# Down-weight sums from GpSimd to VectorE, gated layers' norms from VectorE to ScalarE, token sums pair by pair

## The chip, the cores and the metric

The kernel runs on one core of one Trainium2 chip. The metric is the device time of one execution in microseconds (us). The engines that appear are TensorE (PE, with its weight loads as PEld), VectorE (DVE), ScalarE (ACT), GpSimd (POOL) and SyncE (SP), which issues most transfers. A row of the trace that says L663 belongs to line 663 of the kernel before.

## What is computed

Four layers stand on a residual stream x of 2048 tokens with 1024 features. Layers 0 and 2 are linear attention, layers 1 and 3 are gated feed-forward layers; both kinds use the same two sets of weights. Each layer takes a layer norm of x and adds its result to x.

```
def _layernorm(x, axis=-1, eps=1e-5):          # (x - mean) / sqrt(var + eps)

A:  q, k, v = heads(x @ wqkv)                  # 32 heads of 32
    pq, pk = phi(q), phi(k)                    # t + 1 where t > 0, else exp(t); + 1e-6
    kv = einsum(pk, v);  z = sum(pk)
    o  = einsum(pq, kv) / (einsum(pq, z) + 1e-6)
    return o @ wo

B:  gate = x @ W_gate;  up = x @ W_up          # 1024 -> 3584
    h = relu(gate) * up
    return h @ W_down                          # 3584 -> 1024

x = x + A(layernorm(x));  x = x + B(layernorm(x))
x = x + A(layernorm(x));  x = x + B(layernorm(x))
```

## The kernel before

Tokens are 16 tiles of 128 (t = 0 to 15), four tiles to a quarter. x stays in SBUF in fp32.

**Attention layers** (`layer_A`). After the projections and the key-value product comes the out stage: for each tile and each half of the columns `out_unit` (line 544) runs eight matmuls into a PSUM bank (one of four), and VectorE adds the result to x (line 555). During the out units of quarters 1 and 2 the norms of the next layer's first two quarters are prepared: `ln_at` (line 344) queues, step by step, two statistics on VectorE (line 154), their aggregate (line 159), two short operations on ScalarE for 1/sqrt (lines 161 and 162), the scaling of the whole 128 x 1024 tile on VectorE (`ln_scale`, line 170), and a transposing transfer on SP's queue (`ln_turn`, line 342).

**Gated layers** (`layer_B`). Tokens go in two chunks of eight tiles (c = 0, 1). The three big products use a block scheme with seven block products in place of eight (2 x 2 blocks): so sums of blocks are needed of the tokens (`sums_x`, lines 697 to 700, four VectorE operations for a pair of tiles), of the gate and up weights (`make_gu`, lines 663 to 666, three VectorE operations on a weight block) and of the down weights (`make_d`, lines 670 to 686, four GpSimd operations on a unit). The weights' sums are made once, in layer 1, chunk 0, and are stored to DRAM by transfers on ScalarE's queue (lines 667 and 684); chunk 1 and layer 3 load them.

A chunk has fourteen gate/up units (`glu`, line 708), each of fourteen groups of four matmuls, then one down stage (`down`, line 777). In a unit ScalarE copies products from PSUM (lines 741 and 745) and applies relu (line 732), VectorE joins them (lines 755, 758 and 735; zg and zu are the sums of line 755, on which the next matmuls accumulate), and GpSimd makes one product (line 762).

**Order.** `later.at(n, f)` queues f until n ticks on; a tick is one unit of matmuls in attention, one group of four in a gated layer. In the out stage the order on VectorE and GpSimd is the order of the code (line 599). Elsewhere a planner orders each engine's instructions in advance from estimated costs. Either way every engine and each transfer queue then runs its list strictly in order. SP's queue has the loads and transposes, ScalarE's queue has the stores of the sums. Large buffers come from one pool of 16 (`slot`, line 146): weight blocks in a ring, the token blocks, their sums, h, and the raw down weights with their sums; a load starts when an earlier user has released its buffer.

Of the kernel before, what the change touches and what calls it, by code (L numbers as in the profile page):

```python
# [8 lines left out]
ALU = mybir.AluOpType  # L9
ACT = mybir.ActivationFunctionType  # L10
F32 = mybir.dt.float32
BF16 = mybir.dt.bfloat16
F16 = mybir.dt.float16
PSUM = bass.MemoryType.PSUM
P = 128
NW = 512
HD = 32
QT = 4
# [71 lines left out]
class _Net:  # L90
# [71 lines left out]
        nc.scalar.activation(out=rstd, in_=rstd, func=ACT.Exp, scale=-0.5)  # L162
        return mv, rstd

    def ln_scale(self, src, mv, rstd, xn=None, h=None):
        if xn is None:
            xn = self.temp([P, self.D], F16, name="xnb")
        w = self.D // 2
        s = slice(None) if h is None else slice(h * w, (h + 1) * w)
        self.nc.vector.tensor_scalar(out=xn[:, s], in0=src[:, s], scalar1=mv[:, 0:1],  # L170
                                     scalar2=rstd[:, 0:1], op0=ALU.subtract, op1=ALU.mult)
        return xn

    def ln_norm(self, layer, t):

        nc = self.nc
        src = self.xb[t] if layer == 0 else self.x[t]
        stats = self.small.tile([P, 2, nc.vector.BN_STATS_DIM], F32, tag="stats")
        for c in range(2):
            self.ln_stat(t, src, c, stats)  # L180
        r = self.ln_rstd(stats)

        def scale():
            home = self.xn_home(layer, t) if layer % 2 == 0 else None
            return self.ln_scale(src, *r, home)

        return scale

# [209 lines left out]
    def layer_A(self, l, last_ln):  # L398
        nc, G, KT, D = self.nc, self.G, self.KT, self.D
        ring, later = self.ring, self.later  # L400
        H = D // NW
        heads = lambda a: a.rearrange("p (h d) -> p h d", d=HD)
        pq_of, pqT, T = {}, {}, []
# [52 lines left out]
        def m_units(d):  # L456
            mt = self.temp([P, D], BF16, name=f"mt{l}_{d}")
            for h in range(H):
                ps = self.ps3.tile([P, NW], F32, tag="b")
                for t in range(self.ST):  # L460
                    nc.tensor.matmul(ps, lhsT=self.xn[l, t][:, d * P:(d + 1) * P],  # L461
                                     rhs=self.pk[l, t][:, h * NW:(h + 1) * NW],
                                     start=(t == 0), stop=(t == self.ST - 1))
                    if t == self.ST // 2 - 1:
                        later.tick()
                nc.scalar.activation(out=mt[:, h * NW:(h + 1) * NW], in_=ps, func=ACT.Copy)
                if h == H - 1:
                    later.at(2, lambda: kv_step(d, mt))
                later.tick()
# [30 lines left out]
        def z_mult(sc, j):  # L500
            prod = sums[:, 1 - next(prods) % 2, :]
            nc.gpsimd.tensor_tensor(out=prod, in0=pq_of[sc, j], in1=zrow, op=ALU.mult)  # L502
            later.at(2, lambda: z_sum(prod, sc, j))
# [17 lines left out]
        def fold_wo(n):  # L521

            n2, a = divmod(n, H)
            if n2 == 0:
                T.append(self.slot(f"T{l}_{a}", [P, 4, D]))
            ps = [pool.tile([P, NW], F32, tag=tag, name=f"fold{l}_{n}_{i}") for i, (pool, tag) in
                  enumerate(((self.kvp, "kv0"), (self.kvp, "kv1"), (self.ps3, "b"), (self.ps3, "b")))]
            wo = ring.get((l, f"o{n2}"))
            for b in range(R):
                g = a * R + b  # L530
                for i in range(R):
                    e = slice(i * HD, (i + 1) * HD)
                    nc.tensor.matmul(ps[i][b * HD:(b + 1) * HD, :], lhsT=kvT[e, g, e],
                                     rhs=wo[e, g, :], start=True, stop=True,
                                     tile_position=(i * HD, b * HD))
            for i in range(R):
                g = a * R + i
                dst = T[g // 4][:, g % 4, n2 * NW:(n2 + 1) * NW]
                if g % 2:
                    nc.scalar.activation(out=dst, in_=ps[i], func=ACT.Copy)  # L540
                else:
                    nc.vector.tensor_copy(out=dst, in_=ps[i])
# [16 lines left out]
        def column_major(f, q):  # L559
            return [lambda j=j, c=c: f(q, j, c) for c in range(H) for j in range(QT)]  # L560

        def row_major(f, q):
            return [lambda j=j, c=c: f(q, j, c) for j in range(QT) for c in range(H)]

        def run(*lists):

            n = max(len(u) for u in lists)
            for i in range(n):
                for u in lists:
                    if i < len(u):  # L570
                        u[i]()
                        later.tick()
# [26 lines left out]
        with self.tc.manual_schedule(engines={mybir.EngineType.DVE, mybir.EngineType.Pool}):  # L599
            ring.free_before((l, "v0"))  # L600
            later.at(5, z_row)
            for i in range(11):
                later.at(7 + 2 * i, lambda i=i: z_mult(*divmod(i, QT)))
            for d in range(KT):
                m_units(d)
            if l > 0:
                later.at(1, lambda: [self.bring_back(t) for t in range(self.NS)])
            q3 = row_major(q_unit, self.NQ - 1)
            out0 = column_major(out_unit, 0)

            def with_fold(u, i):
                return lambda: (u(), fold_wo(i // 2) if i % 2 == 0 else None)

            run(q3[:2])
            run([with_fold(u, i) for i, u in enumerate(q3[2:] + out0[:1])])
            run(out0[1:3])
            ring.free_slowly((l, "o0"), later, 2)
            for i in range(11, self.ST):
                later.at(1 + 3 * (i - 11), lambda i=i: z_mult(*divmod(i, QT)))
            run(out0[3:])  # L620
            for sc in range(1, self.NQ):
                if sc < 3:
                    self.ln_later(last_ln, sc - 1, 1, 3, 2)
                run(row_major(out_unit, sc))


# [42 lines left out]

    def make_d(self, u):  # L670

        g = self.nc.gpsimd
        t = self.slot(f"wd{u}")
        raw = t[:, 0:4, :].rearrange("p (h n) f -> p h n f", h=2)
        T = t[:, 4:8, :].bitcast(F16)
        self.nc.sync.dma_start(out=raw, in_=self.wd_v[:, :, u, :].rearrange("p h (n f) -> p h n f", f=NW))

        def sums():
            for o, a, b in ((T[:, 0, :], raw[:, 0, 1, :], raw[:, 0, 0, :]),
                            (T[:, 1, :], raw[:, 1, 1, :], raw[:, 0, 1, :]),  # L680
                            (T[:, 2, :], raw[:, 1, 1, :], T[:, 0, :]),
                            (T[:, 3, :], raw[:, 1, 0, :], T[:, 2, :])):
                g.tensor_tensor(out=o, in0=a, in1=b, op=ALU.subtract)  # L683
            self.later.at(2, lambda: self.nc.scalar.dma_start(out=self.td[:, :, u, :], in_=T))

        self.later.at(6, sums)
# [155 lines left out]
    def layer_B(self, l, final):  # L842
        ring = self.ring
        for c in range(2):
            if c == 0:
                for j in range(QT):
                    self.sums_x(l, c, j)
            hT = []
            first = l == 1 and c == 0
            for u in range(self.U):  # L850
                if u % 2 == 0:
                    hT.append(self.slot(f"h{l}_{c}_{u // 2}", dtype=F16))
                ring.load_to(ring.index((l, c, "g", u)) + (4 if first else 5))
                if first:
                    if u == 0:
                        for w in "gu":
                            self.make_gu(ring.get((l, c, w, 0)), w, 0)
                    if u + 1 < self.U:
                        self.later.at(4, lambda u=u: [self.make_gu(ring.get((l, c, w, u + 1)), w, u + 1)
                                                      for w in "gu"])  # L860
                    self.make_d(u)
                self.glu(l, c, u, hT)
            if c == 0:
                self.ln_chunk(l, 1, 20, 3, 3)
            elif not final:
                self.ln_later(l + 1, 0, 28, 6, 4)
            self.down(l, c, hT, final)
# [68 lines left out]
```

## Time and profile before

| | us |
|---|---|
| median of 3 runs (1545.25 to 1549.07) | 1545.67 |
| the profiled execution | 1544.92 |
| its span, first to last instruction | 1543.0 |
| out stage of layer 0 (180.63 to 247.27) | 66.64 |
| layer 1, chunk 0: gate/up (247.27 to 457.14) | 209.87 |
| layer 1, chunk 0: down (457.14 to 544.67) | 87.53 |
| layer 1, chunk 1: gate/up (544.67 to 713.88) | 169.21 |
| out stage of layer 2 (970.77 to 1032.08) | 61.31 |
| layer 3, chunk 0: gate/up (1032.08 to 1200.87) | 168.79 |
| layer 3, chunk 1: gate/up (1285.47 to 1454.69) | 169.22 |

A row of a group of instructions reads: line, engine, operation, result <- operands, partitions x elements and type, count, then busy us in total, mean ns of one, and the idle time of the engine before them with what ended it. A row of waits reads: engine and what it was about to run, <- what it waited for, then us in total, times, longest. A row of the timeline reads: start, length, engine, line, operation, count, and in brackets the idle time before it.

### The profile page before, as it was taken

To read this page: it belongs to the slowest core of one execution; us is meant where nothing else is said; L and a number is where in the kernel's file an instruction comes from. 1 tells how busy PE (TensorE), PEld (TensorE's weight loads), DVE (VectorE), ACT (ScalarE), POOL (GpSimd) and SP (SyncE) were. 2 spreads that over 40 slices of the span, in tenths; PEclk is the share of its full clock that TensorE was granted. 3 is DMA by queue.
4 is the path that set the end of the run, shared out by engine and by line. 5 is a ranking of instruction groups with operands and counts; after the bars stand their busy time and mean duration, and the time that the engine had idled before them with its cause. 6 is when DMAs were issued, how large, how long until landed. Compare 5 with 4: busy or idle time off the path is not lost.

```text
span 1543.0 us, 18575 instructions
## 1 busy us (share of the span) xinstructions
PE 1487.9 (96%) x6993; PEld 671.9 (44%) x7039; DVE 877.6 (57%) x1399; ACT 464.7 (30%) x875; POOL 349.3 (23%) x246
## 2 busy tenths in 40 slices
PE   9999988788999999999999999989999999999999
PEld 4444433333344444444444444434444444444444
DVE  7845699866666454337356554895334733344632
ACT  5851202233320033342027622123343102433300
POOL 1349244333440001000003377311000000000100
PEclk9999999999999999999999999999999999999999
DMA  9402447655665894444752116576443589444461
GB/s 273 96 28 55 131 69 209 204 174 183 203 202 177 259 326 136 147 150 144 236 136 41 55 21 169 138 181 201 150 150 127 175 221 311 151 137 142 143 205 41
DMA packets 295673, 242.91 MB, mean 157 GB/s; under 512 B 105504, under 2 KB 269600, under 8 KB 295584
## 3 DMA queue, kind: packets, MB, share of 16 engines
q1 hardware_dynamic: 278224, 214.07, 47.5%
q10 hardware_dynamic: 17360, 27.66, 5.0%
q8 instruction: 55, 0.90, 0.2%
q14 instruction: 34, 0.28, 0.0%
HBM read 186.65 MB, written 30.41 MB: 141 GB/s over the span
## 4 chain that ended last, share of the span: by engine, by line
PE 84%; DVE 10%; DMA 3%; issue 2%; POOL 1%; ACT 0%; ACTq 0%; DVEq 0%; SPq 0%; POOLq 0%
PE ps L426 14%; PE dy L807 9%; PE yg L724 9%; PE yu L724 9%; PE ps L461 7%; PE dv L807 6%; PE xu L724 5%; PE xg L724 5%; PE dx L807 5%; PE zg L724 3%; PE zu L724 3%; PE vg L724 3%; PE vu L724 3%; PE ps L548 2%; DVE x L555 1%
## 5 line engine op out<-in xcount | busy, mean ns | idle before, releaser
L724 PEld LDWEIGHTS <-w 128*128 128x128 f16 (+1 forms) x3136 | 308.3, 98 | 413.9 <-issue 46.4
L762 POOL TENSOR_TENSOR h<-m5u,m5g 128x512 f16<-128x512 f32 x56 | 72.1, 1288 | 750.9 <-DVE m5u L758 721.3
L426 PE MATMUL ps<-w,xnT 128*128 128x512 bf16 x1024 | 223.4, 379 | 0.2 <-ACT xnT L286 0.2
L807 PEld LDWEIGHTS <-h 128*128 128x128 f16 x1120 | 109.4, 98 | 132.3
L755 DVE TENSOR_TENSOR zg<-yg,m5g 128x512 f32<-128x512 f32 x56 | 39.1, 698 | 209.1 <-PE yg L724 209.1
L426 PEld LDWEIGHTS <-xnT 128*128 128x128 bf16 x1024 | 99.2, 98 | 120.1 <-issue 1.4
L724 PE MATMUL yg<-s,w 128*128 128x512 f16 x448 | 117.8, 386 | 20.5 <-DVE zg L755 20.5
L548 PE MATMUL ps<-T,pqT 128*128 128x512 bf16 x500 | 112.3, 379 | 10.4 <-DVE x L555 9.5
L724 PE MATMUL xg<-xnT,w 128*128 128x512 f16 x448 | 115.8, 380 | 5.1 <-ACT yg L745 5.1
L724 PE MATMUL xu<-xnT,w 128*128 128x512 f16 x448 | 115.0, 379 | 2.4 <-ACT yu L745 2.4
L724 PE MATMUL yu<-s,w 128*128 128x512 f16 x448 | 116.5, 383 | 0.0
L732 ACT ACTIVATE m5g<-m5g 128x512 f32<-128x512 f32 x56 | 35.2, 629 | 224.0 <-DVE m5g L758 203.7
L807 PE MATMUL dy<-w,h 128*128 128x512 f16 x448 | 98.0, 379 | 0.0
L807 PE MATMUL dx<-w,h 128*128 128x512 bf16 x436 | 96.7, 379 | 0.6
L161 ACT ACTIVATE rstd<-mv,eps 128x1 f32<-128x1 f32 x64 | 18.3, 291 | 254.5 <-DVE mv L159 237.6
L548 PEld LDWEIGHTS <-pqT 128*128 128x128 bf16 x512 | 49.7, 97 | 72.4 <-issue 13.8
L683 POOL TENSOR_TENSOR wd<-wd 128x512 f16<-128x512 bf16 x56 | 73.4, 1333 | 33.1 <-DMA wd<-in_B_W_down_dram 24.8
L741 ACT ACTIVATE m5g<-vg 128x512 f32<-128x512 f32 x56 | 33.4, 597 | 151.0 <-PE vg L724 70.3
L514 POOL TENSOR_TENSOR pq<-pq,den 128x1024 bf16<-128x1024 bf16 x32 | 61.6, 1930 | 71.8 <-DVE den L509 70.5
L154 DVE BATCH_NORM_STATS2 stats<-x 128x6 f32<-128x512 f32 (+1 forms) x120 | 76.7, 673 | 1.9 <-DMA x<-in_A_x_dram 1.5
L502 POOL TENSOR_TENSOR sums<-pq,kvc 128x1024 f32<-128x1024 bf16 x32 | 69.1, 2165 | 31.6 <-DVE pq L374 18.3
L443 POOL TENSOR_TENSOR sums<-sums,slab 128x512 f32<-128x512 f32 x46 | 53.9, 1179 | 78.2 <-DVE slab L374 60.9
(100 smaller groups left out, 1964.1 us busy)
## 6 DMA issues: line engine op xcount, KB each, us to landing
w<-in_B_W_gate_dram SPq DMA_DIRECT2D x56, 512.0 KB, 6.0
w<-in_B_W_up_dram SPq DMA_DIRECT2D x56, 512.0 KB, 5.3
w<-td SPq DMA_DIRECT2D x32, 896.0 KB, 4.6
w<-in_B_W_down_dram SPq DMA_DIRECT2D x24, 896.0 KB, 5.2
w<-tg SPq DMA_DIRECT2D x42, 512.0 KB, 7.1
w<-tu SPq DMA_DIRECT2D x42, 512.0 KB, 6.3
w<-in_A_wqkv_dram SPq DMA_DIRECT2D x10, 1024.0 KB, 6.9
tg<-w ACTq DMA_DIRECT2D x14, 512.0 KB, 3.1
```

The costliest lines, as they stand in the source:

```text
L154: self.nc.vector.bn_stats(out=stats[:, c, :], in_=src[:, c * fmax:(c + 1) * fmax])
L426: nc.tensor.matmul(by_row(ps), lhsT=self.xnT[l, l_q][:, kt, j * P:(j + 1) * P], rhs=w[:, kt, :].rearrange("p (b i d) -> p i b d", i=R, d=H ...
L443: nc.gpsimd.tensor_tensor(out=ksum[:, cols], in0=ksum[:, cols], in1=pk, op=ALU.add)
L461: nc.tensor.matmul(ps, lhsT=self.xn[l, t][:, d * P:(d + 1) * P], rhs=self.pk[l, t][:, h * NW:(h + 1) * NW], start=(t == 0), stop=(t == sel ...
L502: nc.gpsimd.tensor_tensor(out=prod, in0=pq_of[sc, j], in1=zrow, op=ALU.mult)
L514: nc.gpsimd.tensor_tensor(out=heads(pq), in0=heads(pq), in1=den[:, :].unsqueeze(2).to_broadcast([P, D // HD, HD]), op=ALU.mult)
L548: nc.tensor.matmul(ps, lhsT=pqT[sc][:, g, j * P:(j + 1) * P], rhs=T[g // 4][:, g % 4, n2 * NW:(n2 + 1) * NW], start=(g == 0), stop=(g == G ...
L683: g.tensor_tensor(out=o, in0=a, in1=b, op=ALU.subtract)
L724: nc.tensor.matmul(ps, lhsT=W[w][m][:, k, :], rhs=A[m][:, k, :], start=start and k == 0, stop=k == 3, skip_group_check=True)
L755: nc.vector.tensor_tensor(out=Z[w], in0=Y[w], in1=V[w], op=ALU.add)
L762: nc.gpsimd.tensor_tensor(out=h[:, 3, :], in0=V["u"], in1=V["g"], op=ALU.mult)
L807: nc.tensor.matmul(banks[j], lhsT=A(k)[:, j * P:(j + 1) * P], rhs=w[:, i, :], start=start and k == 0, stop=k == self.U - 1, skip_group_che ...
```

## The change

Three things are edited.

1. `make_d` makes its sums with three VectorE operations (the first one makes two blocks at once, 128 x 1024) in place of four GpSimd operations.
2. `ln_norm`: in layers 1 and 3, and for the first quarter of layer 2, the tile is scaled on ScalarE, in one activation with a scale and a bias per token. The bias, -mean / std, is one VectorE operation on 128 x 1 (tile `shift`). Layer 0 and the other tiles of layer 2 stay on VectorE.
3. The token sums of chunk 0 are queued in the out stage, one pair of tiles at a time, 3j + 6 ticks into quarter 2, where before all four followed the out stage. In layer 0 the sums of the first gate and up blocks are queued one tick into quarter 3. Both thereby get a place in VectorE's order as written in the code.

```diff
-    def ln_scale(self, src, mv, rstd, xn=None, h=None):
-        if xn is None:
-            xn = self.temp([P, self.D], F16, name="xnb")
+    def ln_scale(self, src, mv, rstd, xn, h=None):
...
-        r = self.ln_rstd(stats)
+        mv, rstd = self.ln_rstd(stats)
 
         def scale():
-            home = self.xn_home(layer, t) if layer % 2 == 0 else None
-            return self.ln_scale(src, *r, home)
+            if layer % 2 == 0 and (layer, t // QT) != (2, 0):
+                return self.ln_scale(src, mv, rstd, self.xn_home(layer, t))
+            xn = self.temp([P, self.D], F16, name="xnb") if layer % 2 else self.xn_home(layer, t)
+            shift = self.small.tile([P, 1], F32, tag="shift")
+            nc.vector.tensor_scalar(out=shift, in0=mv[:, 0:1], scalar1=rstd[:, 0:1], scalar2=-1.0,
+                                    op0=ALU.mult, op1=ALU.mult)
+            nc.scalar.activation(out=xn, in_=src, func=ACT.Identity, scale=rstd[:, 0:1],
+                                 bias=shift[:, 0:1])
+            return xn
...
             for sc in range(1, self.NQ):
                 if sc < 3:
                     self.ln_later(last_ln, sc - 1, 1, 3, 2)
+                if sc == 2:
+                    for j in range(QT):
+                        later.at(3 * j + 6, lambda j=j: self.sums_x(last_ln, 0, j))
+                if sc == 3 and l == 0:
+                    for w in "gu":
+                        later.at(1, lambda w=w: self.make_gu(ring.get((last_ln, 0, w, 0)), w, 0))
                 run(row_major(out_unit, sc))
...
     def make_d(self, u):
-        g = self.nc.gpsimd
+        v = self.nc.vector
...
         def sums():
-            for o, a, b in ((T[:, 0, :], raw[:, 0, 1, :], raw[:, 0, 0, :]),
-                            (T[:, 1, :], raw[:, 1, 1, :], raw[:, 0, 1, :]),
-                            (T[:, 2, :], raw[:, 1, 1, :], T[:, 0, :]),
-                            (T[:, 3, :], raw[:, 1, 0, :], T[:, 2, :])):
-                g.tensor_tensor(out=o, in0=a, in1=b, op=ALU.subtract)
+            v.tensor_tensor(out=T[:, 0:2, :], in0=raw[:, :, 1, :], in1=raw[:, 0, :, :], op=ALU.subtract)
+            v.tensor_tensor(out=T[:, 2, :], in0=raw[:, 1, 1, :], in1=T[:, 0, :], op=ALU.subtract)
+            v.tensor_tensor(out=T[:, 3, :], in0=raw[:, 1, 0, :], in1=T[:, 2, :], op=ALU.subtract)
             self.later.at(2, lambda: self.nc.scalar.dma_start(out=self.td[:, :, u, :], in_=T))
...
     def layer_B(self, l, final):
         ring = self.ring
         for c in range(2):
-            if c == 0:
-                for j in range(QT):
-                    self.sums_x(l, c, j)
...
                 if first:
-                    if u == 0:
-                        for w in "gu":
-                            self.make_gu(ring.get((l, c, w, 0)), w, 0)
                     if u + 1 < self.U:
```

## The prediction

> **What bounds the kernel now.** I read the page first, then busy time by stage, then TensorE's waits, then the order of work inside the slowest stage.
>
> ```profile
> span 1543.0 us, 18575 instructions
> PE 1487.9 (96%) x6993; PEld 671.9 (44%) x7039; DVE 877.6 (57%) x1399; ACT 464.7 (30%) x875; POOL 349.3 (23%) x246
> ```
>
> TensorE is busy 96% of the span, so only its gaps can be won. The busy time by stage says where they are (columns: stretch, its length, busy time of PE, PEld, DVE, ACT and POOL, granted clock, DMA share, GB/s). The stretches start at the first matmul of each stage: out stage of layer 0, gate/up of layer 1 chunk 0, its down stage, gate/up of layer 1 chunk 1, out stage of layer 2.
>
> ```profile
> 180.63:247.27 66.64, 57.12 (x269) 25.00 (x273) 62.92 (x105) 5.64 (x19) 21.67 (x12) 1.00 0.51 116
> 247.27:457.14 209.87, 180.94 (x782) 78.55 (x783) 147.45 (x200) 63.70 (x117) 83.60 (x65) 0.95 0.58 189
> 457.14:544.67 87.53, 84.51 (x388) 38.28 (x392) 51.25 (x95) 7.19 (x23) 2.33 (x2) 1.00 0.77 235
> 544.67:713.88 169.21, 169.21 (x785) 76.60 (x784) 72.14 (x107) 65.33 (x112) 17.85 (x14) 1.00 0.55 174
> 970.77:1032.08 61.31, 56.64 (x269) 25.02 (x273) 54.72 (x97) 5.65 (x19) 17.17 (x8) 1.00 0.49 111
> ```
>
> The same fourteen gate/up units take 169.2 us where the weights' sums are only loaded, and 209.87 us where they are made: 40.7 us lost. The two out stages lose 66.64 - 57.12 = 9.5 and 61.31 - 56.64 = 4.7 us, and there VectorE is the busy engine. The first down stage loses 3.0 us. Together 57.9 us: what this change could win at most. TensorE's waits in those stretches, first five rows in gate/up of chunk 0, then one row each in the out stage of layer 0 and in the down stage (from the waits of each stretch):
>
> ```profile
> PE yg L724 <- DVE zg L755: 20.5, 6, 4.4
> PE xg L724 <- ACT yg L745: 5.1, 5, 2.0
> PE vg L724 <- DVE s L697: 3.6, 1, 3.6
> PE xu L724 <- ACT yu L745: 2.4, 1, 2.4
> PE yu L724 <- DVE m5u L758: 0.9, 1, 0.9
> PE ps L548 <- DVE x L555: 5.6, 7, 2.5
> PE dv L807 <- DVE x L873: 2.8, 1, 2.8
> ```
>
> The wait for s ends at 247.27 and belongs to the out stage. The others of gate/up give 28.9 us; the remaining 40.7 - 28.9 = 11.8 us must be matmuls at a lower clock (0.95 in that stretch). One burst of this stage in order of time (start, length):
>
> ```profile
> 292.49 0.84 DVE L665 TENSOR_TENSOR w<-w 128x512 f16<-128x512 bf16 x1
> 293.00 10.92 POOL L683 TENSOR_TENSOR wd<-wd 128x512 f16<-128x512 bf16 x8
> ...
> 302.84 1.63 DVE L663 TENSOR_TENSOR w<-w 128x1024 f16<-128x1024 bf16 x1
> 304.50 0.43 DVE L665 TENSOR_TENSOR w<-w 128x512 f16<-128x512 bf16 x1
> 305.31 0.69 DVE L755 TENSOR_TENSOR zg<-yg,m5g 128x512 f32<-128x512 f32 x1
> 306.05 1.87 PE L724 MATMUL yg<-s,w 128*128 128x512 f16 x4 [4.36 <-DVE zg L755]
> 307.71 1.91 PE L724 MATMUL zg<-s,w 128*128 128x512 f16 x4
> ```
>
> While GpSimd makes the down sums of two units (293.0 to 303.9), VectorE's sums of the gate and up weights stretch (line 663 to 1.63 us); the first one after it takes 0.43 us. The operation that TensorE needs (zg) stands behind them, TensorE stops 4.36 us, and its next two groups of four matmuls start 1.66 us apart, where a unit's fourteen groups at 169.2 / 14 us are 0.86 apart. Over the whole run:
>
> ```profile
> L663 DVE TENSOR_TENSOR w<-w x28: 677/1316/1640, 178.8 to 433.4; 128x1024 f16<-128x1024 bf16 x28
> L665 DVE TENSOR_TENSOR w<-w x28: 400/771/1367, 179.8 to 434.1; 128x512 f16<-128x512 bf16 x28
> L683 POOL TENSOR_TENSOR wd<-wd x56: 1149/1328/1607, 241.8 to 456.7; 128x512 f16<-128x512 bf16 x56
> L762 POOL TENSOR_TENSOR h<-m5u,m5g x56: 1263/1270/1593, 259.4 to 1453.3; 128x512 f16<-128x512 f32 x56
> ```
>
> The rows give shortest, median and longest ns. The minima (0.68 and 0.40) are VectorE alone, the maxima are beside GpSimd.
>
> **Part 1: the down sums move to VectorE.** Removed are 56 GpSimd operations, 4 x 1.33 = 5.3 us a unit. Added are three on VectorE in the shapes of lines 663, 665 and 666: 0.68 + 0.41 + 0.41 = 1.50 us a unit (0.41 between the shortest, 0.40, and the 0.43 above), 21.0 in fourteen. The store of the result stays on ScalarE's queue and now waits for VectorE. What the gate and up sums cost in this stage now:
>
> ```profile
> L663 DVE TENSOR_TENSOR w<-w 128x1024 f16<-128x1024 bf16 x25 | 30.6, 1228 | 3.9 <-DMA w<-in_B_W_gate_dram 3.3 <-DMA w<-in_B_W_up_dram 0.5
> L666 DVE TENSOR_TENSOR w<-w 128x512 f16<-128x512 bf16 x25 | 22.0, 881 | 0.5
> L665 DVE TENSOR_TENSOR w<-w 128x512 f16<-128x512 bf16 x25 | 19.1, 767 | 0.3
> ```
>
> That is 71.7 us; alone they would take 25 x 1.50 = 37.5. So VectorE does 37.5 + 21.0 = 58.5 us of sums in place of 71.7: more work, 13 us less time, 147.45 - 13.2 = 134 us for a stage of 169 of TensorE. The burst shows what this does to the wait: from 292.49 to 305.31 VectorE ran three sums like line 663, eight of the short kind and one 0.68 operation, 12.8 us. Alone: 3 x 0.68 + 8 x 0.41 + 0.68 = 6.0, plus the down sums of two units, 3.0, makes 9.0. Zg comes 3.8 us sooner and 0.6 of the 4.36 us stay. With no long stop the lower clock goes too.
>
> What stays of the 40.7: six waits for zg at 0.5 = 3.0; half of the 7.5 us for the copies on ScalarE, which stand behind the issues of the stores (these wait for the sums) = 3.7; the lower clock, 1; and something new. A wait for the down weights' load, which held GpSimd alone, now holds VectorE, and behind it zg, the products into h and, through the stores, ScalarE's copies. In this stage GpSimd's row is 8.9 us:
>
> ```profile
> POOL wd L683 <- DMA wd<-in_B_W_down_dram: 8.9, 2, 8.7
> wd<-in_B_W_down_dram SPq DMA_DIRECT2D x12, 512.0 KB, 4.5
> td<-wd ACTq DMA_DIRECT2D x13, 512.0 KB, 3.7
> ```
>
> I take 6 of it, the rest meeting slack. Residue 14, so 27 us won. Bounds: all 40.7, or below nothing (the slower rival). One conflict stays: the product on GpSimd (line 762) meets VectorE's sums once a unit; I take it as hidden: by the code it follows the unit's last addition, and nine groups of matmuls, some 8 us, lie between that and the next zg. The Trainium skill's page SBUF — State Buffer, "Who interferes with whom" and the rule above it, says that the port pair VectorE and GpSimd share is an exclusive lock, so a two-input VectorE operation can stand for a whole GpSimd operation. By it the sum could lose up to what rival 4 works out, where mine loses nothing; the trace's worst stretch of line 663, 1.64 against 0.68 us, is less than such a full block.
>
> **Part 2: norms scaled on ScalarE.** The rows are line 170 in the out stages of layers 0 and 2, a ScalarE copy of the same width, and the nearest tiny operation:
>
> ```profile
> L170 DVE TENSOR_SCALAR xnb<-x,mv,rstd 128x1024 f16<-128x1024 f32 x8 | 12.0, 1496 | 0.2
> L170 DVE TENSOR_SCALAR xnb<-x,mv,rstd 128x1024 f16<-128x1024 f32 x8 | 10.1, 1257 | 0.2
> L448 ACT ACTIVATE e<-sums 128x1024 bf16<-128x1024 f32 x2 | 2.1, 1047 | 0.0
> L508 DVE TENSOR_SCALAR den<-den 128x32 f32<-128x32 f32 x4 | 0.7, 182 | 0.1
> ```
>
> Each tile takes one VectorE operation of 0.8 to 1.5 us away, adds a shift of at most 0.18 there and some 1.05 us on ScalarE (from nothing hidden to twice that, should scale and shift cost extra). ScalarE is busy 5.64 of 66.64 and 7.19 of 87.53 us in these stages, so that costs nothing; were it busy, the transpose would start 1 us later, still inside its two steps of lag. The out stage of layer 0 has VectorE at 62.92 - 12.0 + 1.4 = 52.3, that of layer 2 at 54.72 - 10.1 + 1.4 = 46.0, both below TensorE's 57. The down stage's wait of 2.8 ends behind eight such operations and goes: 2.8 won (0 to 3.0).
>
> **Part 3: token sums pair by pair, first sums of the weights before the stage.** No operation is added; they get a fixed place on VectorE.
>
> ```profile
> L697 DVE TENSOR_TENSOR s<-xnT 128x512 f16<-128x512 f16 x4 | 3.0, 742 | 0.0
> L548 PE MATMUL ps<-T,pqT 128*128 128x512 bf16 x500 | 112.3, 379 | 10.4 <-DVE x L555 9.5
> xnT<-xnb SPq DMA_TRANSPOSE x8, 3.1
> ```
>
> Without GpSimd's sums beside them, the token sums at 0.74 us fall to about 0.41. The risk is that VectorE now stops where a transpose is late, and behind it the additions that free PSUM (line 555). A unit of eight matmuls is 1.8 us (112.3 / 500 x 8); the sums come two units, 3.6 us, after a transpose that lands in 3.1, and four PSUM banks give about 7 us more. The first two weights' sums (3.0 us), made near 180 us today, now follow at the start of the last quarter; their load is in by then. Parts 2 and 3 together: of 9.5 us I take 6.5 (bounds -3 to 9.5, the low end three late transposes at 1 us each beyond that cover), of 4.7 us 3.5 (-3 to 4.7).
>
> **Sum.** 27 + 6.5 + 3.5 + 2.8 = 39.8. The profiled execution took 1544.92 us and the median of the runs is 0.75 above it: 1544.92 - 39.8 + 0.75 = 1505.9, say 1506.
>
> **Rivals.**
> 1. VectorE waits for the loads (slower). With few buffers free, a unit's down load starts only when the store before it has landed: 4.5 + 1.5 + 3.7 = 9.7 us, or 12.1 (a unit of TensorE) with issue waits. Where it is late VectorE stops some 4.5 us, less 0.9 of slack, and the lower clock adds 3 to 4: about 7.5 us a unit. The stage then loses 7.5 us times such units in place of 40.7; with 12.8 us won elsewhere the balance is even at (40.7 + 12.8) / 7.5, about seven units, and with ten the time is 1545 - 53.5 + 75 = 1567. For it: gate loads already hold VectorE 3.3 us. Against: two such waits in fourteen units.
> 2. Bursts stay. If the planner puts the down sums too between the sums and zg where TensorE has no slack, waits fall only by half, to 20 us lost: 6 less won, and half of the out stages', about 1517.
> 3. The transfers set the pace. The stage moves 189 GB/s x 209.87 us = 39.7 MB; 169 us would want 235, which the down stage just reaches. At 205 it lasts 194 and wins 16: about 1517.
> 4. The product on GpSimd (line 762) now starts on time in every unit and stops a sum of VectorE for its whole 1.27 us, and the delay reaches zg: 14 x 1.27 = 17.8, so 1524. For it: the stretched maxima. Against: 8 us of distance. The page named in part 1 has this rule.
> 5. It does nothing: other waits, all of them on the stores' issues in ScalarE's queue, replace these: 1545.
>
> **How the numbers follow.** Forecast 0.47, bursts or transfers 0.24, the lock 0.08, nothing 0.06, slower 0.15. The range is 1487 (all 57.9 us) to 1543: it leaves out most of the slower cases and half of the case of nothing. The likeliest case's own range is 1490 to 1517. A measurement of this kernel can tell about 0.3% (4.6 us) from no change. Faster by more: 0.47 + 0.24 + 0.08 + a little of the others = 0.81; within: 0.06; slower: 0.13, as the smallest cases of the slower rival still end even.
>
> **What would show it.** Part 1: lines 663, 665 and 666 near 0.68 and 0.41 us, zg waits under 8 us in total, gate/up of chunk 0 of layer 1 near 183 us at a clock of 1.00. Part 2: line 170 gone from the gated layers, waits for line 555 under 4 us over both out stages. Part 3: no wait for s at the first gate matmul. The forecast is wrong if VectorE waits for the down weights' load for more than 15 us, or if sums alone on VectorE still take over 1 us.

## The result and the profile after

The changed kernel takes 1501.82 us (median of 4 runs, 1500.37 to 1502.49) beside 1545.46 of the kernel before on the same chip: a ratio of 0.9712 (95% interval 0.9695 to 0.9729), 43.6 us less. The forecast was 1506 in a range of 1487 to 1543. Its total is near; the parts are not, as the experiments show.

The busy time by stage of the kernel after (columns as before; rows: out stage of layer 0, gate/up of layer 1 chunk 0, its down stage, out stage of layer 2, gate/up of layer 3 chunk 0). Each stage here starts at its first gate/up matmul of any kind:

```profile
180.45:243.44 62.99, 57.15 (x267) 25.30 (x272) 54.30 (x115) 15.85 (x29) 15.82 (x8) 0.97 0.45 111
243.44:417.20 173.76, 170.13 (x785) 76.49 (x785) 128.01 (x241) 66.61 (x119) 17.80 (x14) 1.00 0.72 235
417.20:501.80 84.60, 84.34 (x388) 38.33 (x392) 47.02 (x93) 14.61 (x28) 0.30 (x1) 1.00 0.77 239
927.90:986.34 58.44, 55.89 (x267) 24.89 (x271) 49.07 (x103) 15.96 (x29) 15.82 (x8) 1.00 0.55 128
986.34:1157.25 170.91, 170.91 (x785) 77.14 (x785) 79.55 (x130) 66.40 (x118) 17.82 (x14) 0.99 0.49 156
```

By the same boundaries the kernel before has these rows:

```profile
180.63:243.10 62.47, 56.53 (x267) 24.90 (x272) 58.75 (x101) 5.64 (x19) 17.92 (x10) 1.00 0.46 102
243.10:457.14 214.04, 181.53 (x785) 78.65 (x784) 151.62 (x204) 63.70 (x117) 87.35 (x68) 0.95 0.59 192
970.77:1031.13 60.36, 56.05 (x266) 24.91 (x271) 53.77 (x94) 5.65 (x19) 17.17 (x8) 1.00 0.48 108
1031.13:1200.87 169.74, 169.39 (x786) 76.51 (x785) 81.53 (x130) 66.93 (x120) 17.86 (x14) 1.00 0.52 164
```

Gate/up of layer 1 chunk 0 wins 214.04 - 173.76 = 40.3 us (the 214.04 hold the wait for s of 3.6, which the prediction counted in the out stage), the down stage behind it 87.53 - 84.60 = 2.9. The out stage of layer 0 loses 0.5, that of layer 2 wins 1.9, of which gate/up behind it gives 1.2 back. Together 43.4 of the 43.6 us between the two spans (1543.0 and 1499.4). So nearly everything comes from the one stage; VectorE has 4 to 5 us less to do in each out stage, and these stages hardly move.

TensorE's waits over the whole run of the kernel after, those above 1 us behind the head (line 553 was 548, 733 was 724, 560 was 555, 764 was 755, 706 was 697):

```profile
PE ps L553 <- DVE x L560: 5.0, 3, 4.1
PE yg L733 <- DVE zg L764: 3.5, 2, 2.0
PE vg L733 <- DVE s L706: 2.0, 1, 2.0
```

The wait for zg fell from 20.5 to 3.5 us and the waits for ScalarE's copies, 7.5 before, are gone. The sums in gate/up of chunk 0, from the groups of that stretch (the first three are gate and up, the others the down weights):

```profile
L674 DVE TENSOR_TENSOR w<-w 128x1024 f16<-128x1024 bf16 x24 | 16.7, 697 | 3.6 <-DMA w<-in_B_W_gate_dram 2.0 <-DMA w<-in_B_W_up_dram 1.6
L676 DVE TENSOR_TENSOR w<-w 128x512 f16<-128x512 bf16 x24 | 12.5, 522 | 0.1
L677 DVE TENSOR_TENSOR w<-w 128x512 f16<-128x512 bf16 x24 | 10.0, 415 | 0.2
...
L690 DVE TENSOR_TENSOR wd<-wd 128x1024 f16<-128x1024 bf16 x13 | 8.9, 685 | 8.0 <-DMA wd<-in_B_W_down_dram 8.0
...
L691 DVE TENSOR_TENSOR wd<-wd 128x512 f16<-128x512 bf16 x13 | 5.4, 416 | 0.1
```

With line 692, another 5.4 us, all sums together take 58.9 us, where the gate and up sums alone took 71.7. Alone, at 1.50 us a set, these 24 + 13 sets would take 55.5; four gate and up sets and one down set run ahead of the stage.

Why the out stage of layer 0 wins nothing is to be read in its timeline (the last part of quarter 2 and quarter 3):

```profile
224.27 0.42 DVE L706 TENSOR_TENSOR s<-xnT 128x512 f16<-128x512 f16 x1 [2.99 <-DMA xnT<-xnb]
...
229.64 0.69 DVE L674 TENSOR_TENSOR w<-w 128x1024 f16<-128x1024 bf16 x1
...
233.80 0.68 DVE L690 TENSOR_TENSOR wd<-wd 128x1024 f16<-128x1024 bf16 x1
...
235.41 0.68 DVE L560 TENSOR_TENSOR x<-x,ps 128x512 f32<-128x512 bf16 x1
...
236.14 1.44 PE L553 MATMUL ps<-T,pqT 128*128 128x512 bf16 x3 [4.07 <-DVE x L560]
```

VectorE first stands 3.0 us for the transposes of the first pair of token tiles. Then a block of sums, 229.2 to 235.4 (a pair's token sums, those of three weight blocks and two of the first down block's three), runs ahead of the addition that frees a PSUM bank, and TensorE stops 4.07 us.

### The profile page after: what moved, and what is told of

Same layout as the page of the kernel before. It is cut to its first block, busy times and chain, and to the rows that moved or that the text cites. A ratio compares the mean times of both kernels' runs of the same rounds, so it can differ in the third digit from the quotient of the medians.

```text
span 1499.4 us, 18590 instructions
## 1 busy us (share of the span) xinstructions
PE 1479.0 (99%) x6993; PEld 671.6 (45%) x7039; DVE 830.2 (55%) x1441; ACT 508.3 (34%) x911; POOL 274.2 (18%) x190
## 4 chain that ended last, share of the span: by engine, by line
PE 92%; DVE 4%; DMA 2%; issue 1%; ACT 0%; POOL 0%; SPq 0%; DVEq 0%; ACTq 0%; POOLq 0%
PE ps L431 14%; PE dy L816 10%; PE yg L733 10%; PE yu L733 10%; PE ps L466 7%; PE dv L816 6%; PE dx L816 6%; PE xg L733 6%; PE xu L733 6%; PE ps L553 3%; PE zg L733 3%; PE zu L733 3%; PE vg L733 3%; PE vu L733 3%; DVE stats L154 1%; DVE x L560 1%
## 5 line engine op out<-in xcount | busy, mean ns | idle before, releaser
L379 DVE SCALAR_TENSOR_TENSOR pq<-ps,e 128x512 bf16<-128x512 f32 x64 | 43.9, 686 | 46.9 <-ACT e L373 45.2
L816 PEld LDWEIGHTS <-e 128*128 128x128 f16 x448 | 43.8, 98 | 52.9
```

What stands on the lines that cost most here:

```text
L379: nc.vector.scalar_tensor_tensor(out=out, in0=ps, scalar=0.0, in1=e, op0=ALU.max, op1=ALU.add)
L816: nc.tensor.matmul(banks[j], lhsT=A(k)[:, j * P:(j + 1) * P], rhs=w[:, i, :], start=start and k == 0, stop=k == self.U - 1, skip_group_che ...
```

## The experiments

On the chips used the kernel before took 1545.5 to 1548.3 us (medians), so each kernel is compared by its ratio to the kernel before on the same chip.

| kernel | parts | ratio | 95% interval | median us | gate/up, chunk 0 |
|---|---|---|---|---|---|
| changed kernel | 1, 2, 3 | 0.9712 | 0.9695 to 0.9729 | 1501.82 | 173.76 |
| e1 | 2, 3 | 1.0005 | 0.9988 to 1.0021 | 1547.70 | 208.78 |
| e2 | 1 | 0.9706 | 0.9658 to 0.9754 | 1501.76 | 171.94 |
| e5 | 1, 3 | 0.9763 | 0.9747 to 0.9780 | 1510.74 | 172.34 |
| e6 | 1, 2 | 0.9659 | 0.9634 to 0.9683 | 1493.83 | 174.38 |
| e7 | 1, 2, half of 3 | 0.9674 | 0.9660 to 0.9688 | 1497.75 | 173.34 |
| e8 | e7, token sums a tick later | 0.9637 | 0.9623 to 0.9651 | 1492.68 | 176.00 |
| e9 | e8, norms closer | 0.9624 | 0.9598 to 0.9649 | 1489.69 | 173.18 |

**e1: part 1 undone.** Edit:

```diff
 def sums():
-    v.tensor_tensor(...)   # three on VectorE
+    g.tensor_tensor(...)   # four on GpSimd, as before
```

> The changed kernel with the down sums back on GpSimd, in four operations. Theory C (GpSimd's reads stretch VectorE's sums) and theory L (GpSimd's sums are long, so their stores, buffers and ScalarE's queue are late) both expect the gate/up stage of layer 1, chunk 0 back at 200 to 208 us and a time of 1530 to 1540 us, since parts 2 and 3 alone are worth some 7 us. If the gate/up stage stays under 185 us, the gain of that stage came from parts 2 and 3 and both theories fall.

Measured: 1547.70 us, ratio 1.0005. The stage is back at 208.78, near what both theories said (200 to 208), but parts 2 and 3 alone win nothing, where 7 us had been expected. Its gate/up and down stages:

```profile
246.31:455.09 208.78, 180.36 (x784) 78.45 (x784) 143.52 (x201) 63.85 (x115) 83.61 (x65) 0.95 0.60 194
455.09:548.34 93.25, 87.40 (x388) 39.02 (x392) 46.66 (x93) 15.99 (x31) 2.33 (x2) 0.96 0.71 220
```

The down stage takes 93.25 us, 5.7 more than before any change. Its timeline shows a price of part 2 that the forecast had at nothing:

```profile
456.18 0.52 ACTq L695 DMA_DIRECT2D td<-wd  x1
...
474.18 1.24 ACT L188 ACTIVATE xnb<-x,shift,rstd 128x1024 f16<-128x1024 f32 x1 [9.18 <-DVE shift L186]
475.32 0.57 ACT L826 ACTIVATE dy<-dx 128x512 f32<-128x512 f32 x1
...
475.95 4.42 PE L818 MATMUL dx<-w,h 128*128 128x512 bf16 x10 [5.59 <-ACT dy L826]
```

ScalarE's queue holds a scaling, which waits for VectorE's shift, and behind it a copy of PSUM that TensorE needs. VectorE was late here since it had waited 4.4 us for the last store of the down sums. ScalarE was idle, but idle is not free: its list is in order. With part 1 in place VectorE is on time and the wait does not arise (84.60 us).

**e2: part 1 alone.** The kernel before with the three VectorE operations in `make_d` (as in the change) and nothing else.

> The kernel before with the down sums on VectorE in three operations, nothing else changed. Both theories expect the gate/up stage of layer 1, chunk 0 at 172 to 178 us and a time of 1507 to 1512 us: the out stages keep their losses (9.5 and 4.7 us) and the first down stage its 2.8. If the parts need each other (VectorE too full with the norms and the sums), the stage stays above 185 us and the time above 1520.

Measured: 1501.76 us, as fast as the whole change and 5 us below the range expected. Its stages (out stage of layer 0, gate/up, down, out stage of layer 2):

```profile
180.98:244.08 63.10, 57.88 (x266) 25.36 (x271) 59.31 (x103) 5.64 (x19) 16.58 (x8) 0.97 0.47 104
244.08:416.02 171.94, 170.69 (x785) 76.55 (x784) 130.89 (x244) 66.16 (x120) 17.87 (x14) 1.00 0.73 240
416.02:500.63 84.61, 84.35 (x389) 38.34 (x392) 52.01 (x95) 5.58 (x20) 0.31 (x1) 1.00 0.76 237
926.72:987.72 61.00, 57.25 (x267) 25.45 (x272) 54.34 (x95) 5.65 (x19) 17.16 (x8) 0.97 0.47 109
```

Two losses that the prediction gave to parts 2 and 3 go with part 1 alone: the wait for s before the first gate group (the first down sums had run on GpSimd beside the last token sums), and the down stage's 2.8 us, although VectorE still does the eight scalings there: its wait for the store of the last down sums, 4.2 us at the head of the down stage before the change, does not arise.

**e3: GpSimd reads beside VectorE.** The question is whether the stage was slow because GpSimd's reads stretch VectorE's sums (theory C) or because GpSimd's results came late (theory L). Here GpSimd does work whose results nobody reads, though its product and the next load into the buffer stand behind it; all computations of the kernel are kept.

```diff
     v.tensor_tensor(...)   # the three sums
+    for i in range(16):
+        c = slice((i // 4) * P, (i // 4 + 1) * P)
+        self.nc.gpsimd.tensor_tensor(out=self.ident, in0=raw[:, (i // 2) % 2, i % 2, c],
+                                     in1=raw[:, 1, 1, c], op=ALU.subtract)
```

> The changed kernel; beside VectorE's down sums GpSimd also does sixteen subtractions a unit on 128 x 128 blocks of the same raw weights, some 5 us, into a scratch block that nobody reads. No wait on VectorE or of a store hangs on them. Theory C: lines 674 to 692 go up to 1.0 us and more in the mean, gate/up of layer 1, chunk 0 goes to 190 to 205 us and the time to 1520 to 1535. Theory L: the sums and the stores come as early as in the changed kernel, so the stage stays at 172 to 178 us and the time under 1508.

Measured: 1521.53 us, ratio 0.9834 (0.9787 to 0.9881); gate/up 191.83 us, as theory C expected and not theory L. The stage, then the sums' durations (shortest, median, longest ns):

```profile
245.87:437.70 191.83, 174.05 (x785) 77.36 (x784) 144.92 (x241) 64.89 (x119) 118.36 (x219) 0.98 0.65 213
L674 DVE TENSOR_TENSOR w<-w x28: 678/882/914, 180.9 to 411.0; 128x1024 f16<-128x1024 bf16 x28
L677 DVE TENSOR_TENSOR w<-w x28: 411/614/645, 184.6 to 412.6; 128x512 f16<-128x512 bf16 x28
```

The median is 0.20 us above the shortest for both widths, less than the "1.0 us and more" expected: these operations were small, 128 elements where the down sums have 512. VectorE is busy 144.92 - 128.01 = 16.9 us longer than in the changed kernel and the stage lasts 18.1 us longer. That is under half of the 40 us: e3 shows that the reads slow the stage, and whether late results alone would have cost part of the rest was not tested.

**e4: GpSimd writes only, without a link to the sums.**

```diff
     v.tensor_tensor(...)   # the three sums
+    for i in range(26):
+        self.nc.gpsimd.memset(self.ident, 0.0)
```

> The changed kernel with GpSimd as busy as in the run with the reads (26 memsets of 128 x 128 a unit, some 5 us) but only writing. Theory C, read side: VectorE's sums stay at 0.68 and 0.42 us, gate/up at 172 to 178 us, time 1501 to 1506. If any busy GpSimd stretches VectorE, or if the product on GpSimd behind the extra work is what hurts, this run looks like the one with the reads: 1520 to 1535.

Measured: 1533.63 us, ratio 0.9914 (0.9873 to 0.9954), and it tells nothing on the question. The memsets have no input, so the planner put them into layer 0, ahead of GpSimd's sums of the keys, and the copy of these (line 453) came late:

```profile
PE ps L456 <- ACT e L453: 30.4, 1, 30.4
```

Gate/up itself took 170.33 us in this run.

**e3b and e4b: reads and writes behind the same sums.** Both put their GpSimd work behind the unit's sums, into a raw block that is no longer used, and so hold its buffer; one reads, the other only writes. They were meant to hold it equally long, but the writes were shorter than the reads: without the product, GpSimd was busy 60.51 - 17.80 = 42.7 us with them and 89.11 - 17.80 = 71.3 with the reads (rows below).

```diff
     v.tensor_tensor(...)   # the three sums
+    for i in range(11):    # e3b
+        self.nc.gpsimd.tensor_tensor(out=raw[:, 0, 0, c], in0=raw[:, 0, 1, c], in1=raw[:, 1, 1, c], ...)
+    for i in range(22):    # e4b
+        self.nc.gpsimd.memset(raw[:, 0, 0, c], 0.0)
```

> The changed kernel with eleven GpSimd subtractions a unit (128 x 128, from the raw down weights into a raw block no longer used), each set behind VectorE's three down sums of that unit, so that it holds the buffer some 5 us longer. Theory C (reads of GpSimd stretch VectorE's sums): sums that meet them take some 0.23 us more, as in the first run with reads; only the next unit's sums meet them, so gate/up of layer 1, chunk 0 is at 178 to 190 us and the time at 1506 to 1518. If only the held buffer counts, this run and the one that writes are alike.

> The same with 22 GpSimd memsets of 128 x 128 a unit into the same raw block behind the same sums: the buffer is held and GpSimd is busy as long, but it reads nothing. Theory C, read side: sums stay at 0.68 and 0.41 us, gate/up at 173 to 177 us, time 1501 to 1506. If any GpSimd work stretches VectorE: sums some 0.2 us longer and times as in the run that reads. If the held buffer counts: 178 us and more with short sums.

Measured: with reads 1510.14 us (ratio 0.9757, 0.9714 to 0.9801), with writes 1503.53 (0.9715, 0.9679 to 0.9750). Gate/up with reads, then the line of sums that most often met them:

```profile
245.33:429.81 184.48, 172.55 (x786) 77.10 (x785) 139.30 (x240) 66.91 (x119) 89.11 (x157) 0.99 0.69 221
```

```profile
L676 DVE TENSOR_TENSOR w<-w x28: 407/642/892, 183.8 to 406.5; 128x512 f16<-128x512 bf16 x28
```

and with writes:

```profile
243.35:418.92 175.57, 171.91 (x785) 77.03 (x785) 128.15 (x241) 66.73 (x119) 60.51 (x300) 0.99 0.71 233
```

```profile
L676 DVE TENSOR_TENSOR w<-w x28: 407/411/893, 182.1 to 395.6; 128x512 f16<-128x512 bf16 x28
```

The median of line 676 is 0.64 us with reads and 0.41 with writes; the stage takes 184.5 and 175.6, against 173.8 in the changed kernel. In total times the two intervals overlap (two runs of each, and the trace with reads is of its slower run); the durations and the stage tell them apart. With reads VectorE is busy 11.3 us longer than in the changed kernel and the stage lasts 10.7 us longer. With writes VectorE's time is unchanged, and GpSimd's being busy and the buffer held for longer cost 1.8 us; for the time that the reads take an estimate in proportion, 1.8 x 71.3 / 42.7, gives 3. So GpSimd's reads are what slows the sums, and most of what slows the stage in e3b. The page SBUF — State Buffer of the Trainium skill, "Who interferes with whom", states just this: two-input VectorE operations contend with GpSimd operations that read SBUF and not with those that only write. These runs agree.

**e5: part 2 undone.** All norms are scaled on VectorE (line 170 as before), parts 1 and 3 stay.

```diff
-    nc.vector.tensor_scalar(out=shift, ...); nc.scalar.activation(out=xn, in_=src, ...)
+    return self.ln_scale(src, mv, rstd, xn)
```

> The changed kernel with the norms of all layers scaled on VectorE again (part 2 undone). Theory V (VectorE's load bounds the out stages): VectorE goes up by some 8 x 1.0 us in each out stage, to 62 of 63 and 57 of 58 us, and the time to 1508 to 1518. Theory W (what counts is the order in VectorE's queue: waits for late transposes and blocks of sums ahead of the additions): within 3 us of the changed kernel, 1499 to 1505.

Measured: 1510.74 us, ratio 0.9763. Theory V had this right: VectorE's load in the out stages does count when the token sums have fixed places in them.

```profile
180.65:250.68 70.03, 60.40 (x266) 26.01 (x271) 64.37 (x116) 6.14 (x21) 16.59 (x8) 0.93 0.44 103
933.74:995.56 61.82, 57.51 (x266) 25.33 (x271) 55.09 (x97) 5.64 (x19) 17.16 (x8) 0.97 0.50 119
```

**e6: part 3 undone.** The token sums and the first weights' sums go back to the start of the gated layer, where the planner places them.

```diff
-    later.at(3 * j + 6, lambda j=j: self.sums_x(last_ln, 0, j))     # in the out stage
-    later.at(1, lambda w=w: self.make_gu(ring.get((last_ln, 0, w, 0)), w, 0))
+    self.sums_x(l, c, j)                                            # in layer_B, c == 0
+    self.make_gu(ring.get((l, c, w, 0)), w, 0)                      # in layer_B, u == 0
```

> The changed kernel with part 3 undone: token sums and the first weights' sums at the start of the gated layer again, where the planner places them. Theory V: VectorE has room now that the norms are away, so nothing is lost: 1499 to 1504. Theory W: VectorE's stop for the transposes (3.0 and 2.5 us) and the block of sums (4.1 us of TensorE) go, so the out stages win 3 to 6 us: 1495 to 1499. If pair by pair is needed, the wait for s comes back at the first gate group, 3 to 4 us a layer: 1505 to 1510.

Measured: 1493.83 us, ratio 0.9659, better than the changed kernel. Three of its four runs took 1492.8 to 1493.8 us and one 1501.17. Both out stages come close to TensorE's own time:

```profile
180.48:237.04 56.56, 55.41 (x266) 24.91 (x271) 51.03 (x108) 15.46 (x27) 15.81 (x8) 1.00 0.52 114
922.13:978.53 56.40, 55.41 (x266) 24.91 (x270) 47.83 (x100) 15.97 (x29) 15.81 (x8) 1.00 0.57 132
```

So beside the other parts, part 2 wins (0.9763 - 0.9712) x 1546 = 7.9 us and part 3 costs (0.9712 - 0.9659) x 1546 = 8.2 us; both pairs of intervals lie apart. Neither theory alone covers the runs: the load (V) and the places in the queue (W) count both. Without part 3 the worth of part 2 is not clear of noise: e2 and e6 differ by (0.9706 - 0.9659) x 1546 = 7.3 us, but their intervals overlap.

**e7, e8, e9: which half of part 3, and a better place.** e7 undoes only the move of the first weights' sums; e8 queues the token sums one tick later as well; e9 sets the norms of the second quarter two ticks apart.

```diff
-    later.at(1, lambda w=w: self.make_gu(...))          # e7: back in layer_B
-    later.at(3 * j + 6, ...sums_x...)
+    later.at(3 * j + 7, ...sums_x...)                   # e8
-    self.ln_later(last_ln, sc - 1, 1, 3, 2)
+    self.ln_later(last_ln, sc - 1, 1, 2 if sc == 2 else 3, 2)
+    later.at(2 * j + 7, ...sums_x...)                   # e9
```

> The changed kernel, only the first gate and up sums back in the gated layer, token sums still pair by pair. Theory W: the block of 5.8 us of sums at 229.6 to 235.4 breaks up, TensorE's wait of 4.1 us there goes, time 1496 to 1499. If the block comes from the planner's other sums (unit 1 and the first down sums), nothing changes: 1500 to 1503.

> As the run with the first sums back, and the token sums one tick (1.8 us) later. Theory W: VectorE's stop for the first pair's transposes, 3.0 and 2.5 us, shrinks to some 1 us; TensorE's waits for line 560 fall under 2 us in both out stages; but the last pair ends nearer to the first gate group, so the wait for s of 2.0 us in layer 2 may grow by up to 1.8. Time 1494 to 1499; without an effect of the transposes it equals the run before it.

> As the run with the token sums one tick later, but the norms of the second quarter follow each other at two ticks in place of three and the token sums at two, so that the last pair is summed three ticks (5 us) earlier. Theory W: the wait for s at the first gate groups (2.8 us over both layers) goes, and no new one comes as long as VectorE keeps up in quarter 2: 1488 to 1492. If VectorE falls behind in quarter 2 (its load, theory V), waits for line 560 come back: 1493 to 1498.

Measured: e7 1497.75 us (0.9674), e8 1492.68 (0.9637), e9 1489.69 (0.9624). The wait of 4.07 us for line 560 is gone in e7, so that the moved sums made the block. One tick more for the transposes then wins 0.9674 - 0.9637, 5.7 us, more than expected: the out stages go from 59.90 and 58.45 to 55.75 and 55.51 us, of which gate/up of layer 1 gives 2.7 back. e9 takes the wait for s away too, as expected, but waits for line 560 of 2.5 us come back, and its ratio is within e8's interval. Its stages (out stage of layer 0, gate/up of layer 1 chunk 0, out stage of layer 2):

```profile
180.11:237.25 57.14, 55.88 (x273) 25.10 (x272) 52.53 (x113) 15.76 (x29) 15.81 (x8) 1.00 0.57 130
237.25:410.43 173.18, 169.89 (x785) 76.72 (x784) 128.66 (x243) 66.22 (x119) 17.53 (x14) 1.00 0.71 234
920.93:978.06 57.13, 55.88 (x274) 25.10 (x272) 49.55 (x105) 15.75 (x29) 15.82 (x8) 1.00 0.56 132
```

e6 to e9 are faster than both kernels: their intervals end at 0.9688 or below, that of the changed kernel begins at 0.9695. The intervals of e8 and e9 overlap that of e6, so no run shows that a fixed place for the token sums is better than the planner's.

## Why the prediction was right, and where it was not

**Part 1, the mechanism: right.** GpSimd's reads stretched VectorE's sums, and with them gone VectorE does more sums in less time: 58.9 us measured in the stage, 58.5 forecast (55.5 for the sets that stayed in it). e3 tells this from late results, e3b and e4b from a busy GpSimd and a held buffer.

**Part 1, the residue: mis-sized.** "Residue 14, so 27 us won": measured is 173.76 - 169.2 = 4.6 us of residue. The 3.7 for ScalarE's copies was nothing: with short sums the stores' issues no longer hold its queue, and ScalarE's own waits for VectorE's gate and up sums fell from 22.3 us in the stage to 1.1. The 3.0 for zg behind the sums came to nothing as well: the two waits for zg that came, 3.5 us in all, both follow a wait of VectorE for loads, 1.6 us for an up block at the first, 1.1 for a down block and 2.0 for a gate block at the second. So they belong to the term of 6 for the down load, which was the largest miss: VectorE did wait 8.0 us for it (four times, close to GpSimd's 8.9 before), but most of that found TensorE with other work to do, and the loads of gate and up blocks counted as much. The second wait for zg, from the gate block on:

```profile
385.38 0.69 DVE L674 TENSOR_TENSOR w<-w 128x1024 f16<-128x1024 bf16 x1 [2.04 <-DMA w<-in_B_W_gate_dram]
...
387.65 1.02 PE L733 MATMUL yg<-s,w 128*128 128x512 f16 x4 [2.05 <-DVE zg L764]
```

**Parts 2 and 3 in the out stages: wrong.** "Of 9.5 us I take 6.5 ..., of 4.7 us 3.5." The step that failed is in part 3: that the transposes, landing in 3.1 us, would be covered by two units and by four PSUM banks. VectorE stood 3.0 us there, and the moved weights' sums, to which the text gave no price, became a block that cost TensorE 4.07 us. Two of the signs that the prediction named fail with it: the waits for the additions are 5.0 us, not under 4, and a wait for s of 2.0 us stays in layer 3. Part 2 was worth some 8 us beside part 3, part 3 cost about as much, and the sum was near nothing: e2 without either is as fast. Neither stage fell to the low bound of -3.

**The down stage: right number, wrong owner.** 2.8 us were forecast for part 2 and 2.9 came, but e2 has them with part 1 alone. What made VectorE late was its wait for the store of the last down sums, not the eight scalings, and e1 shows that the scalings on ScalarE make it worse while that store is late.

**The sum.** 39.8 us were forecast and 43.6 measured: 13 too little in gate/up (3.6 of them the wait for s, which the prediction had in the out stage) and some 10 too much around it. That 1506 lies within 5 us of the result is luck in so far as these two balance; the range and the direction would have held with either alone, at about 1493 or 1516.

**Rivals.** Waiting for loads cost TensorE the two waits above, 3.5 us in all, not 7.5 us a unit. (In that rival the 3 to 4 us for the lower clock behind a stop are high: the prediction's own 11.8 us over the five stops above 3.5 us give 2.4 each.) Transfers did not set the pace: the stage ran at 235 GB/s, the rate that rival 3 asked for. The product, now GpSimd's only work in the stage, stretches line 676 in some units (mean 0.52 us against 0.41 alone, longest 0.90), some 3 us of VectorE in all, not 17.8.

## What to carry to other kernels

Look at what an engine's work does to its neighbour before counting its own time: 5.3 us a unit on an engine that bound nothing cost the stage 40 us, for the most part, as far as these runs tell, through reads that slowed another engine's queue. An idle engine or a free slot is no reason by itself: every list is in order, so a moved operation brings its waits to whatever stands behind it, and an early place for a sum is only good if its inputs have landed. Where a change has several parts, run them alone: here one part carried all of it, and of the two others one hid the worth of the other.

## What was not expected of the hardware

The stretch of a VectorE sum is nearly a constant, not a factor. Beside GpSimd's down sums (512 elements in bf16, 1.33 us) the longest were 1.64 for 0.68 and 1.37 for 0.40, both 0.96 to 0.97 more. Beside the subtractions of 128 elements (0.46 us in e3) the longest were 0.91 for 0.68 and 0.65 for 0.41, both 0.23 to 0.24 more, and the medians both 0.20 more. So the time added does not go with the length of the VectorE sum but with what GpSimd does. The length of the GpSimd operation alone does not set it either: the product takes 1.27 us (512 elements in fp32) and stretched line 676 in the changed kernel to 0.90 at most, 0.49 more. In none of these did a sum grow by a whole GpSimd operation. That each sum waits once, for a part of the operation beside it, is argued, not shown.

Short gaps can cost the clock too. In the changed kernel the first gate group of layer 3 follows a gap of 1.97 us:

```profile
986.34 1.70 PE L733 MATMUL vg<-s,w 128*128 128x512 f16 x4 [1.97 <-DVE s L706]
987.83 1.92 PE L733 MATMUL xg<-xnT,w 128*128 128x512 f16 x4
```

The two start 1.49 us apart in place of 0.86, at a granted clock of 0.60 from 986.3 to 990.6. The same gap of 1.97 us before the same group has this effect in e3 too (granted clock 0.63) and not in e1 (1.00). A gap of 2.46 us in the out stage of layer 0 had none before the change, one of 2.47 at the same place in e2 had it (0.60); every gap above 3.5 us in these traces has it, at 0.50 to 0.68 over the next 4.3 us. The page TensorE: Matmul & The Clock Gate of the Trainium skill, Part 1, names about 3.4 us of idle; these traces agree for the long gaps, and the shorter ones show that such a length is no safe limit.
